# Reordering the first attention batch, tile 0's stores and tile 1's plan in a fused attention and feed-forward kernel

## The chip, the cores and the metric

The kernel runs on one core of one Trainium2 chip. The metric is device time in microseconds of that core. The engines are TensorE (PE; its weight loads are a row of their own, PEld), VectorE (DVE), ScalarE (ACT), GpSimd (POOL) and SyncE (SP), which here only issues DMAs. POOL and ACT issue some DMAs too.

## The reference

Sliding-window attention for 8 batches of 8 heads, 576 positions of 64 features, is followed by a two-layer feed-forward network with a tanh GELU:

```python
scores = scale * np.matmul(q, k.transpose(0, 1, 3, 2))
mask = np.abs(pos[:, None] - pos[None, :]) <= 32
scores = np.where(mask, scores, -1000000000.0)
scores = scores - np.max(scores, axis=-1, keepdims=True)
attn = np.exp(scores)
attn = attn / (np.sum(attn, axis=-1, keepdims=True) + 1e-09)
attn_out = np.matmul(attn, v)                       # (8, 8, 576, 64)
x = attn_out.transpose(0, 2, 1, 3).reshape(4608, 512)
h = x @ w_in                                        # 512 -> 2048
g = 0.5 * h * (1.0 + np.tanh(c * (h + 0.044715 * h * h * h)))
return g @ w_out                                    # 2048 -> 512, float32
```

All inputs and the output are float32; the products on PE are made in float16.

## The kernel before, in words

**Tiles.** The 4608 tokens of the network are cut into nine tiles of 512, counted by `t`. Tile `t` reads the end of batch `t - 1` and the beginning of batch `t` from a ring buffer `xT`, and the attention of batch `b = t + 1` is woven into tile `t`, most of it into its second matrix product. Batch 0 comes first, by itself.

**Attention of one batch.** There are four groups `g = 0..3`, one for each pair of heads, over most of the query positions, and a "tail" group (4, written `-1` when it is done one tile later) for the last positions of all heads. The steps of a group have one letter each in the plans: `s` scores and exp (`score`, PE L415, ACT L427), `m` multiply by the band (DVE L433), `v` sums and products with V (`weigh`: PE L438 and L448, then ACT L473 and L474, a Ln and an Exp that make the reciprocal of the sum), `x` the scaled write into `xT` (`spread`, DVE L483 or L489). For batch 1, `n` and `p` are the sums and the products of two groups at once, `d` copies a chunk of V to the paired layout (`pair_chunk`, DVE L198 and L200), `w` and `u` cast chunks of w_out, `c` is a `combine` (see below).

**Order.** The order on every engine is the order in which the program issues the instructions; nothing is rescheduled. `PLAN_0`, `PLAN_1` and `PLAN` say which attention step is put ahead of which matmul `i` of the second matrix product of tile 0, tile 1 and the rest ("@0" and "@1" name the PSUM tile S0 or S1 that a step uses).

**Feed-forward of one tile.** `ffn_in(t, fc)` makes one of 16 hidden columns with four matmuls (PE L520, out to one of a few PSUM banks) and calls `gelu` (ACT L528). From tile 1 on, the second product is done by a Strassen-Winograd scheme: `sums` (DVE L563) makes four combinations of GELU's outputs after every fourth column, `combine` (DVE L553) makes the combinations T1 to T4 of w_out once, and `ffn_out` runs 112 matmuls (PE L618). Its first product needs eight GELU outputs of every second column. Tile 0 uses a plain product (`ffn_out_0`, PE L592, w_out cast in L218); its four results of 128 tokens (`t4` = 0..3) are copied out of PSUM in L598 and put into the list `later` in the order 0, 3, 1, 2. Results 0 and 1 go to halves of one tile `yo2`, which is in the pool `hp` with the tag "qt16"; `hp` has one buffer for each tag. Results 2 and 3 go to two buffers "yo". ACT stores 0 and 3 to HBM at `i` = 61 and 62, POOL stores 1 and 2 after the loop (L582).

**Batch 2 in tile 1.** `load_qk(2)` puts q and k on SP's queue. `cast_and_turn(2)` casts q on DVE (L343), issues its transposing DMA from SP (L346), then casts k (L367), issues two more transposing DMAs (L369) and the four loads of V (L375), and does combine 2 before the keys and 3 and 4 after them. It returns `rest`, which is called in five steps after columns 9 to 13: four casts of the query tail on ACT into `qt16` (L351, also tag "qt16" of `hp`), the key tail on ACT (L357), and two transposing DMAs and a load on SP. POOL casts V chunk by chunk (`cast_v`, L294), issued after columns 3 to 6. The loads of batch 3 follow on SP.

**The start.** Batch 0 is cast and transposed on PE, pair by pair (`turn`, `trans_out`), with idle matmuls (`spin`, L240) between. `sums_of` makes the sums and reciprocals of a group; `times` multiplies by V for the slots it is given, where slots 0 to 3 are chunks of V and 4 to 7 pair the halves of two neighbours (7 holds the tail). The last chunk is cast by POOL, and ACT and DVE copy halves of it (L730, L729). Then w_in is cast (L218) and the first `ffn_in` starts.

Of the kernel before, what the change touches and what calls it, by code (L numbers as in the profile page):

```python
# [36 lines left out]
def cut(b):  # L37
# [14 lines left out]

PLAN_0 = {8: "r2@0", 10: "s0@1", 11: "w1", 14: "s1@0", 18: "t-1@1", 21: "r3@1", 22: "m0 s2@0", 25: "s3@1", 26: "m1",
          29: "s-1@0", 30: "w2", 31: "m2", 32: "m3", 33: "n0@1", 36: "m-1", 38: "n2@0", 42: "d0", 43: "d1", 44: "v-1@1",
          46: "w3", 48: "x-1", 49: "d2", 51: "d3", 54: "p0@0", 55: "u3 p2@1 x0 x1", 56: "x2 x3", 60: "c1"}
PLAN_1 = PLAN | {10: "s0@0", 12: "s1@1", 33: "s2@0", 40: "v0@1 v1", 50: "x0", 53: "x1", 58: "s-1@1", 62: "s3@0 v2",
                 64: "m-1", 66: "m3", 74: "v-1@1", 76: "x2", 80: "x-1", 86: "s4@1", 91: "v3", 98: "m4"}
PLAN_1[16] = "m0 m1"
for i in (4, 44, 84):
    del PLAN_1[i]  # L60
PAIR_1 = {17: slice(0, 4), 40: slice(4, 8)}

# [9 lines left out]
def kernel(  # L72
# [132 lines left out]
    def stage_w():  # L205
        return stage.tile([128, 4, 512], FP32, name="wst", tag="stage")

    def load_w_in(i, w, c0=0, c1=4):
        nc.sync.dma_start(w[:, c0:c1, :], w_in_v[:, c0:c1, 512 * i:512 * i + 512])  # L209
        return w  # L210
# [17 lines left out]
    vs(4, 0, 1, 2, 3)  # L228
    wi = []
    for i in range(4):  # L230
        wi.append(load_w_in(i, stage_w(), 0, 2))
        load_w_in(i, wi[i], 2, 4)

    idle = KTs[1][:, 0, 0:512]
    nc.vector.memset(idle, 0.0)
# [99 lines left out]
    def cast_and_turn(b):  # L335
        cast_open(b)
        q16, k16 = halfs[b]
        qr, kr, qt, kt = raws[b]
        qt16 = hp.tile([16, NPAIR, 4, 2, 64], FP16, name="qt16", tag="qt16")
        kt16 = hp.tile([64, NPAIR, 2, 64], FP16, name="kt16", tag="t16")  # L340
        def queries(src, dst, p0, p1):
            for pr in range(NPAIR):
                nc.vector.tensor_copy(  # L343
                    dst[:, pr, :, :, :].rearrange("p j h d -> p h j d"),
                    src[:, 2 * pr:2 * pr + 2, :].rearrange("p h (j d) -> p h j d", j=4))
            nc.sync.dma_start_transpose(QTs[b].rearrange("d r j p -> d (r j) p")[:, :, p0:p1],  # L346
                                        dst.rearrange("p r j h d -> p (r j h d)"))

        def rest(i):
            if i < NPAIR:  # L350
                nc.scalar.copy(qt16[:, i, :, :, :].rearrange("p j h d -> p h j d"),  # L351
                               qt[:, 2 * i:2 * i + 2, :].rearrange("p h (j d) -> p h j d", j=4))
            if i == 3:
                nc.sync.dma_start_transpose(QTs[b].rearrange("d r j p -> d (r j) p")[:, :, 128:144],
                                            qt16.rearrange("p r j h d -> p (r j h d)"))
            if i == 4:
                nc.scalar.copy(kt16.rearrange("p r h d -> p (r h d)"), kt.rearrange("p h d -> p (h d)"))  # L357
                nc.sync.dma_start_transpose(
                    KLs[b % 2], kt16.rearrange("p r h d -> p (r h d)"))
                raws[b].append(tailp.tile([64, H, 64], FP32, name="vt", tag="vt"))  # L360
                nc.sync.dma_start(raws[b][4], v[b, :, 512:S, :].rearrange("h p d -> p h d"))

        queries(qr, q16, 0, 128)
        if b == 2:
            combine(2, nc.vector)
        for pr in range(NPAIR):
            nc.vector.tensor_copy(k16[:, pr, :, :, :], kr[:, :, 2 * pr:2 * pr + 2, :])  # L367
            if pr % 2:
                nc.sync.dma_start_transpose(  # L369
                    KTs[b % 2][:, pr - 1:pr + 1, :].rearrange("d r (c p) -> d (r c) p", c=4),  # L370
                    k16[:, pr - 1:pr + 1, :, :, :].rearrange("p r c h d -> p (r c h d)"))
        if b == 2:
            vr = rawp.tile([128, 4, H, 64], FP32, name="qr")
            for c in range(4):
                nc.sync.dma_start(vr[:, c, :, :],  # L375
                                  v[b, :, 128 * c:128 * c + 128, :].rearrange("h p d -> p h d"))
        if b == 2:
            combine(3, nc.vector)
            combine(4, nc.vector)
            raws[b] = [None, None, None, vr]  # L380
            return rest
        queries(qt, qt16, 128, 144)
        nc.vector.tensor_copy(kt16.rearrange("p r h d -> p (r h d)"), kt.rearrange("p h d -> p (h d)"))
        nc.sync.dma_start_transpose(
            KLs[b % 2], kt16.rearrange("p r h d -> p (r h d)"))
# [296 lines left out]
    cast_early(0, 0, split)  # L682
    turn(0)
    trans_out(0, 0, *pts[0], nc.scalar.copy)
    cast_tails(0, nc.vector, odd)
    spin(3)
    trans_tails(0, psO.tile([128, 8, 128], FP16, name="pt", tag="O"), odd, nc.scalar.copy)
    cast_early(0, 1, split)
    spin(1)
    score(0, 0, 0)  # L690
    turn(1)
    cast_early(0, 2, split)
    trans_out(0, 1, *pts[1], nc.scalar.copy)
    spin(1)
    turn(2)
    cast_early(0, 3, split)
    trans_out(0, 2, *pts[2])
    score(0, 1, 1)
    cast_vt(0)
    sums_of(0)  # L700
    spin(1)
    score(0, 2, 0)
    turn(3)
    trans_out(0, 3, *pts[3])
    score(0, 3, 1)
    sums_of(1)
    cast_v(0, 0)
    cast_v(0, 1)
    pair_chunk(0, 0, nc.vector.tensor_copy)
# [7 lines left out]

    cast_v(0, 2)
    pair_chunk(0, 2, nc.vector.tensor_copy)
    sums_of(2)  # L720
    os[0], os[1] = bank(0), bank(1)
    s0 = psS.tile([128, 2, 512], FP32, name="ps_o", tag="S0")
    os[2], os[3] = s0[:, 0, :], pieces("S1", "ps_o")
    spin(2, 512, s0[:, 1, :])
    for g in range(3):
        times(0, g, os[g], groups[(0, g)], (0, 1, 2, 4, 5))
    spin(1, 512, s0[:, 1, :])
    cast_v(0, 3)
    nc.vector.tensor_copy(Vs[0][odd, 7, :, :], raws[0][3][odd, 3, :, :])  # L729
    nc.scalar.copy(Vs[0][even, 6, :, :], raws[0][3][even, 3, :, :])  # L730
    sums_of(3)
    times(0, 3, os[3], groups[(0, 3)], (0, 1, 2, 4, 5))
    spin(3, 512, s0[:, 1, :])
    for g in range(4):
        times(0, g, os[g], groups.pop((0, g)), (3, 6, 7))
        spread(0, g, os[g], lts[g])
    for c in range(4):
        cast_w(wi[0], w_in16[:, :, 0:512], (3,), (c,))
    spin(2, 512, pieces("D", "spin"))
    cast_w(wi[1], w_in16[:, :, 512:1024], (0, 2))  # L740
    for dc in range(2):
# [51 lines left out]
    for t in range(NT):  # L793
        b = t + 1
        att = b < B
        if t:
            for fc in range(begun):
                ffn_in(t, fc, 3, 4, then=False)
            for fc in range(begun):
                gelu(t, fc)  # L800
            if att and b > 1:
                rest = cast_and_turn(b)
            for fc in range(begun, NF):
                ffn_in(t, fc)
                if t == 1 and fc in (3, 4, 5, 6):
                    cast_v(2, fc - 3)
                if t == 1 and 9 <= fc < 14:
                    rest(fc - 9)
                if t == 1 and fc == 8:
                    trans_tails(1, psO.tile([128, 8, 128], FP16, name="pt", tag="O"))  # L810
                if t > 1 and fc == 8 and att:
                    pair_v(b, nc.vector.tensor_copy)
        plan = PLAN_0 if not t else PLAN_1 if t == 1 else PLAN if att else {5: "v-1", 31: "x-1"} if t == B - 1 else {}

        def group(g):
            return (b, g) if g >= 0 else (b - 1, 4)
# [6 lines left out]
        for i in range(113 if t else 65):  # L823
# [3 lines left out]
            for act in plan.get(i, "").split():  # L827
# [33 lines left out]
                elif kind == "u":  # L861
                    cast_w(wo[g], w_out16[:, 12:16, :], on_dve=(3,), cs=(2, 3))
                    cast_tails(1, nc.gpsimd)
                    load_qk(2)
                elif kind == "c":
                    if g == 1:
                        B12 = combine_w()
                    combine(g, nc.vector)
                elif kind == "s":
                    score(*group(g), at)  # L870
                elif kind == "d":
                    pair_chunk(b, g, nc.vector.tensor_copy)
                elif kind == "m":
                    mask(*group(g))
                elif kind == "v":
                    bb, gg = group(g)
                    o, d = weigh(bb, gg, at)
                    ods[g] = (o, invert(bb, gg, d))
                    if t and g < 0 and b + 1 < B:
                        load_vt(b + 1)  # L880
                    if t and g == (3 if att else -1):
                        load_table(gelu_set)
                else:
                    spread(*group(g), *ods[g])
            if t == 1 and i == 30:
                cast_vt(2)
            if t == 1 and i in PAIR_1:
                pair_v(2, nc.vector.tensor_copy, PAIR_1[i])
            if t == 0 and i in (61, 62):
                store(0, *later.pop(0), slice(0, 512), nc.scalar)  # L890
            if t == 0 and i < 64:
                ffn_out_0(*ORDER_0[i])
            elif t and i < 112:
                ffn_out(t, i)
        if t == 0:
            for t4, yo in later:
                store(0, t4, yo)
            wino_rest(B12)
            load_table(gelu_set)
        else:  # L900
            ffn_last(t)
# [31 lines left out]
```

## Time and profile before

| | us |
|---|---|
| median of 13 runs | 304.63 |
| lowest, highest run | 301.81, 306.49 |
| the profiled execution's own time | 304.63 |
| its span, first to last instruction | 302.9 |
| PE busy | 289.6 (96%) |
| DVE busy | 193.2 (64%) |
| ACT busy | 193.8 (64%) |
| POOL busy | 91.3 (30%) |

The profile is one execution. "Busy" counts the engine's own instructions, not the waits on DMAs or the issuing of them. A line of a timeline gives start, duration, engine, source line, operation, output and input, the number of instructions merged, and in brackets the idle time ahead of it with what ended it. "SPq" and "ACTq" are DMA issues on these engines' queues. The first `ffn_in` begins at 19.7 us, tile 0's second product at 35.4, tile 1 at 57.8, tile 1's second product at 71.8 and tile 2 at 91.2.

### The profile page before, as it was taken

The page shows a single profiled execution, that of the slowest core. Times are in us where ns is not written, and L with a number is a line of the kernel's source. Part 1 is how long each engine was busy: PE and PEld are TensorE (multiplying, and loading weights), DVE is VectorE, ACT ScalarE, POOL GpSimd, SP SyncE. Part 2 cuts the span into 40 slices and gives each one's busy share as a digit, 9 for nine tenths or more (in the row PEclk, how much of TensorE's full clock was granted, in tenths as well). Part 3 has the DMA queues.
Part 4 walks back from the last instruction along what each step waited for, and adds up shares of the span by engine and source line. Part 5 has one row for each costly group of instructions (what it writes and reads, how often), then busy time and mean ns, then how long its engine had stood idle before and what let it go on. Part 6 is the DMA issues. An engine that isn't in the chain of part 4 may idle for free.

```text
span 302.9 us, 7124 instructions
## 1 busy us (share of the span) xinstructions
PE 289.6 (96%) x2898; PEld 180.0 (59%) x2898; DVE 193.2 (64%) x434; ACT 193.8 (64%) x307; POOL 91.3 (30%) x142
## 2 busy tenths in 40 slices
PE   8899899899999999999999999999997999999993
PEld 3444443446674488448844884488546864784583
DVE  4554556969768686958685869576955635543452
ACT  4776778389775796579657956695666666706600
POOL 3446426201626050605080506050800050015000
PEclk9999999999999999999999999999999999999998
DMA  7999999999799999799979997999594031004013
GB/s 217 247 358 376 329 267 268 275 250 193 204 186 170 168 240 151 147 153 230 160 153 145 229 160 166 139 228 161 86 172 45 3 92 49 2 3 137 2 40 99
DMA packets 116550, 50.73 MB, mean 167 GB/s; under 512 B 97911, under 2 KB 109943, under 8 KB 116518
## 3 DMA queue, kind: packets, MB, share of 16 engines
q1 hardware_dynamic: 87332, 37.88, 60.0%
q0 software_dynamic: 27776, 10.83, 25.4%
q10 hardware_dynamic: 1410, 1.58, 1.6%
q8 instruction: 22, 0.36, 0.5%
q14 instruction: 10, 0.08, 0.1%
HBM read 36.70 MB, written 9.44 MB: 152 GB/s over the span
## 4 chain that ended last, share of the span: by engine, by line
PE 68%; DMA 18%; SPq 7%; DVE 3%; POOL 1%; issue 1%; ACT 0%
PE mm L618 30%; PE mm L520 17%; PE ph L520 13%; DMA wst<-in_moe_w_out_dram 6%; DMA wst<-in_moe_w_in_dram 4%; DMA KT<-k 3%; PE ps_s L415 3%; SPq L175 2%; PE ps_d L438 2%; DMA kr<-in_k_dram 2%; DMA qr<-in_v_dram 2%; SPq L151 2%; SPq L209 2%; DMA tr<-in_k_dram 2%; PE ps_o L448 2%
## 5 line engine op out<-in xcount | busy, mean ns | idle before, releaser
L520 PEld LDWEIGHTS <-w_in 128*128 128x128 f16 x576 | 56.2, 98 | 66.6 <-POOL w_in L218 0.6
L520 PE MATMUL mm<-xT,w_in 128*128 128x512 f16 x304 | 74.7, 379 | 0.1
L528 ACT ACTIVATE gT<-mm 128x512 f16<-128x512 f32 x76 | 45.2, 598 | 38.9 <-PE mm L520 38.2
L520 PE MATMUL ph<-xT,w_in 128*128 128x512 f16 x272 | 68.2, 379 | 0.1
L582 POOL DMA_DIRECT2D out_dram<-y x55 | 32.9, 605 | 90.4 <-DVE y L647 81.7
L618 PEld LDWEIGHTS <-s 128*128 128x128 f16 x512 | 49.5, 98 | 6.0
L563 DVE TENSOR_TENSOR s<-gT 128x512 f16<-128x512 f16 x64 | 27.2, 425 | 34.2 <-ACT gT L528 34.1
L528 ACT ACTIVATE gT<-ph 128x512 f16<-128x512 f32 x68 | 37.9, 599 | 13.5 <-PE ph L520 13.5
L618 PE MATMUL mm<-t,s 128*128 128x256 f16 x376 | 45.1, 273 | 0.0
L618 PEld LDWEIGHTS <-gT 128*128 128x128 f16 x384 | 35.8, 98 | 6.7
L427 ACT ACTIVATE pe<-ps_s 128x960 f16<-128x960 f32 (+1 forms) x32 | 30.5, 976 | 14.0 <-PE ps_s L415 13.9
L618 PE MATMUL mm<-w_out,gT 128*128 128x256 f16 x256 | 33.2, 273 | 0.0
L97 ACT ACT_TABLE_LOAD x17 | 21.8, 1283 | 2.2 <-issue 1.9
L474 ACT ACTIVATE lt<-lt 128x480 f32<-128x480 f32 (+3 forms) x36 | 21.1, 585 | 1.1
L473 ACT ACTIVATE lt<-ps_d 128x480 f32<-128x480 f32 (+2 forms) x28 | 15.5, 554 | 7.9 <-PE ps_d L438 4.6
L433 DVE TENSOR_TENSOR pe<-pe,band 128x960 f16<-128x960 f16 x28 | 18.8, 695 | 1.1 <-ACT pe L427 1.1
L183 POOL DMA_DIRECT2D V<-in_v_dram x20 | 17.9, 909 | 1.4 <-PE ps_o L448 1.0
L448 PEld LDWEIGHTS <-V 128*64 128x64 f16 x520 | 14.0, 111 | 6.5 <-DVE V L200 1.2
L618 PE MATMUL mm<-t,gT 128*128 128x256 f16 x128 | 16.5, 273 | 0.0
L415 PE MATMUL ps_s<-QT,KT 64*64 64x128 f16 (+3 forms) x576 | 13.8, 216 | 2.4 <-DMA KT<-k 1.8
L415 PEld LDWEIGHTS <-KT 64*64 64x64 f16 x576 | 10.1, 106 | 8.6 <-issue 4.9
L618 PE MATMUL mm<-w_out,s 128*128 128x256 f16 x120 | 14.4, 273 | 0.0
(107 smaller groups left out, 325.3 us busy)
## 6 DMA issues: line engine op xcount, KB each, us to landing
kr<-in_k_dram SPq DMA_DIRECT2D x31, 256.0 KB, 10.9
qr<-in_q_dram SPq DMA_DIRECT2D x6, 1024.0 KB
wst<-in_moe_w_in_dram SPq DMA_DIRECT2D x8, 512.0 KB, 9.3
wst<-in_moe_w_out_dram SPq DMA_DIRECT2D x3, 1024.0 KB, 10.7
V<-in_v_dram POOLq DMA_DIRECT2D x20, 128.0 KB, 8.4
vr<-in_v_dram SPq DMA_DIRECT2D x8, 256.0 KB, 5.4
qr<-in_q_dram SPq DMA_DIRECT2D x7, 256.0 KB, 4.3
out_dram<-y POOLq DMA_DIRECT2D x6, 192.0 KB, 6.1
```

The source lines that it names most:

```text
L97: nc.scalar.add_instruction(mybir.InstLoadActFuncSet(name=nc.get_next_instruction_name(), act_func_set_id=which, ins=[], outs=[]))
L183: nc.gpsimd.dma_start(V[:, c, :, :], v[b, :, 128 * c:128 * c + 128, :].rearrange("h p d -> p h d"))
L415: nc.tensor.matmul(ps[64 * half:64 * half + 64, h, 4 * n * r:4 * n * r + 4 * n].rearrange("k (j p) -> k j p", j=4)[:, :, p0 - q0:p1 - q0], ...
L427: nc.scalar.activation(pe, ps[:, :, 0:w], AF.Exp, scale=SCALE)
L433: nc.vector.tensor_tensor(pe, pe, m.rearrange("k (o j) p -> k o j p", o=1).broadcast_to(list(pe.shape)), op=ALU.mult)
L448: nc.tensor.matmul(o[64 * h:64 * h + 64, cols].rearrange("d (j p) -> d j p", j=4)[:, :, p0 - q0:p1 - q0], Vs[b % 2][:, slot, 2 * pr + h, : ...
L474: nc.scalar.activation(lt[:, 0:n], lt[:, 0:n], AF.Exp, scale=-1.0)
L520: nc.tensor.matmul(ph, w_in16[:, dc, fc * 128:fc * 128 + 128], xT[:, dc, t * 512 % RING:t * 512 % RING + 512], start=(dc == 0), stop=(dc = ...
L528: nc.scalar.activation(gTs[t][:, fc, :], phs[fc], AF.Gelu_apprx_tanh)
L563: nc.vector.tensor_tensor(dst, x, y, op=op)
L582: eng.dma_start(out_v[b, j, q0 + p:q0 + p + e, cols], yo[m:m + e, cols])
L618: nc.tensor.matmul(pys["apart"][:, 0:256] if apart else py[:, blk, :], lhsT, wino[w][:, f, :], start=(new and i % (8 if one else 16) == 0) ...
```

## The change

Seven edits are made together.

1. The first attention: scores are issued ahead of some copies, sums later, and the products with V in three steps (slots 0, 1, 4; then 2, 5; then 3, 6, 7); fewer idle matmuls; DVE casts the last chunk and copies its half from the cast V. One chunk of the first w_in cast goes from POOL to ACT.
2. The loads of w_in are written as a loop.
3. `PLAN_0`: `d2` and `d3` come ahead of `x-1`.
4. `cast_and_turn(2)`: combine 3 comes ahead of the keys; the keys, their transposes, the loads of V and combine 4 come after column 3; `qt16` and `kt16` are allocated when first used.
5. `cast_v` of batch 2 comes after columns 6 to 9 and not 3 to 6.
6. Tile 0's stores come in tile 1: ACT's two after columns 5 and 6, POOL's two after column 7.
7. `PLAN_1`: `s-1`, `m-1` and `v-1` one step earlier; `v3` ahead of the tail's score `s4`, and the GELU table's load after that score's exp.

```diff
 PLAN_0 = {8: "r2@0", ...
-          46: "w3", 48: "x-1", 49: "d2", 51: "d3", 54: "p0@0", 55: "u3 p2@1 x0 x1", 56: "x2 x3", 60: "c1"}
-PLAN_1 = PLAN | {10: "s0@0", 12: "s1@1", 33: "s2@0", 40: "v0@1 v1", 50: "x0", 53: "x1", 58: "s-1@1", 62: "s3@0 v2",
-                 64: "m-1", 66: "m3", 74: "v-1@1", 76: "x2", 80: "x-1", 86: "s4@1", 91: "v3", 98: "m4"}
+          46: "w3", 48: "d2", 50: "d3", 52: "x-1", 54: "p0@0", 55: "u3 p2@1 x0 x1", 56: "x2 x3", 60: "c1"}
+PLAN_1 = PLAN | {10: "s0@0", 12: "s1@1", 33: "s2@0", 40: "v0@1 v1", 50: "x0", 53: "x1", 57: "s-1@1", 62: "s3@0 v2",
+                 63: "m-1", 66: "m3", 73: "v-1@1", 76: "x2", 80: "x-1", 86: "v3", 90: "s4@1", 98: "m4"}
 PLAN_1[16] = "m0 m1"
-for i in (4, 44, 84):
+for i in (4, 44, 84, 91):
     del PLAN_1[i]
...
     for i in range(4):
-        wi.append(load_w_in(i, stage_w(), 0, 2))
-        load_w_in(i, wi[i], 2, 4)
+        wi.append(stage_w())
+        for c0 in (0, 2):
+            load_w_in(i, wi[i], c0, c0 + 2)
...
-        qt16 = hp.tile([16, NPAIR, 4, 2, 64], FP16, name="qt16", tag="qt16")
-        kt16 = hp.tile([64, NPAIR, 2, 64], FP16, name="kt16", tag="t16")
+        small = {}
+        def tails_of(which):
+            if which not in small:
+                small[which] = hp.tile([16, NPAIR, 4, 2, 64], FP16, name="qt16", tag="qt16") if which == "q" else \
+                    hp.tile([64, NPAIR, 2, 64], FP16, name="kt16", tag="t16")
+            return small[which]
...
         def rest(i):
+            qt16, kt16 = tails_of("q"), tails_of("k") if i == 4 else None
...
+        def keys():
+            for pr in range(NPAIR):
+                nc.vector.tensor_copy(k16[:, pr, :, :, :], kr[:, :, 2 * pr:2 * pr + 2, :])
+                if pr % 2:
+                    nc.sync.dma_start_transpose(...)
+            if b == 2:
+                vr = rawp.tile([128, 4, H, 64], FP32, name="qr")
+                for c in range(4):
+                    nc.sync.dma_start(vr[:, c, :, :],
+                                      v[b, :, 128 * c:128 * c + 128, :].rearrange("h p d -> p h d"))
+                raws[b] = [None, None, None, vr]
         queries(qr, q16, 0, 128)
         if b == 2:
             combine(2, nc.vector)
-        for pr in range(NPAIR):
-            ...
-        if b == 2:
             combine(3, nc.vector)
-            combine(4, nc.vector)
-            raws[b] = [None, None, None, vr]
-            return rest
+            return keys, rest
+        keys()
...
     cast_early(0, 0, split)
     turn(0)
     trans_out(0, 0, *pts[0], nc.scalar.copy)
+    cast_early(0, 1, split)
     cast_tails(0, nc.vector, odd)
     spin(3)
-    trans_tails(0, psO.tile([128, 8, 128], FP16, name="pt", tag="O"), odd, nc.scalar.copy)
-    cast_early(0, 1, split)
-    spin(1)
+    trans_tails(0, psO.tile([128, 8, 128], FP16, name="pt", tag="D"), odd, nc.scalar.copy)
     score(0, 0, 0)
     turn(1)
     cast_early(0, 2, split)
-    trans_out(0, 1, *pts[1], nc.scalar.copy)
+    trans_out(0, 1, *pts[1])
     spin(1)
+    sums_of(0)
+    cast_early(0, 3, split)
     turn(2)
-    cast_early(0, 3, split)
+    score(0, 1, 1)
     trans_out(0, 2, *pts[2])
-    score(0, 1, 1)
     cast_vt(0)
-    sums_of(0)
     spin(1)
     score(0, 2, 0)
     turn(3)
     trans_out(0, 3, *pts[3])
+    sums_of(1)
     score(0, 3, 1)
-    sums_of(1)
+    sums_of(2)
...
-    sums_of(2)
     os[0], os[1] = bank(0), bank(1)
     s0 = psS.tile([128, 2, 512], FP32, name="ps_o", tag="S0")
-    os[2], os[3] = s0[:, 0, :], pieces("S1", "ps_o")
-    spin(2, 512, s0[:, 1, :])
+    os[2] = s0[:, 0, :]
     for g in range(3):
-        times(0, g, os[g], groups[(0, g)], (0, 1, 2, 4, 5))
-    spin(1, 512, s0[:, 1, :])
-    cast_v(0, 3)
-    nc.vector.tensor_copy(Vs[0][odd, 7, :, :], raws[0][3][odd, 3, :, :])
+        times(0, g, os[g], groups[(0, g)], (0, 1, 4))
+    sums_of(3)
+    os[3] = pieces("S1", "ps_o")
+    times(0, 3, os[3], groups[(0, 3)], (0, 1, 4))
+    spin(3, 512, s0[:, 1, :])
+    for g in range(4):
+        times(0, g, os[g], groups[(0, g)], (2, 5))
+    cast_v(0, 3, nc.vector.tensor_copy)
+    nc.vector.tensor_copy(Vs[0][odd, 7, :, :], Vs[0][odd, 3, :, :])
     nc.scalar.copy(Vs[0][even, 6, :, :], raws[0][3][even, 3, :, :])
-    sums_of(3)
-    times(0, 3, os[3], groups[(0, 3)], (0, 1, 2, 4, 5))
-    spin(3, 512, s0[:, 1, :])
     for g in range(4):
         times(0, g, os[g], groups.pop((0, g)), (3, 6, 7))
         spread(0, g, os[g], lts[g])
     for c in range(4):
-        cast_w(wi[0], w_in16[:, :, 0:512], (3,), (c,))
+        cast_w(wi[0], w_in16[:, :, 0:512], (3,), (c,), (1,))
...
             if att and b > 1:
-                rest = cast_and_turn(b)
+                parts = cast_and_turn(b)
             for fc in range(begun, NF):
                 ffn_in(t, fc)
-                if t == 1 and fc in (3, 4, 5, 6):
-                    cast_v(2, fc - 3)
+                if t == 1 and fc == 3:
+                    parts[0]()
+                    combine(4, nc.vector)
+                if t == 1 and fc in (5, 6):
+                    store(0, *later.pop(0), slice(0, 512), nc.scalar)
+                if t == 1 and 6 <= fc < 10:
+                    cast_v(2, fc - 6)
+                if t == 1 and fc == 7:
+                    while later:
+                        store(0, *later.pop(0))
                 if t == 1 and 9 <= fc < 14:
-                    rest(fc - 9)
+                    parts[1](fc - 9)
...
                     score(*group(g), at)
+                    if t == 1 and g == 4:
+                        load_table(gelu_set)
...
-                    if t and g == (3 if att else -1):
+                    if t > 1 and g == (3 if att else -1):
                         load_table(gelu_set)
...
-            if t == 0 and i in (61, 62):
-                store(0, *later.pop(0), slice(0, 512), nc.scalar)
...
         if t == 0:
-            for t4, yo in later:
-                store(0, t4, yo)
             wino_rest(B12)
```

More of the change, by code (lines that the diff above doesn't have):

```diff
@@ L361, in rest @@
                 nc.sync.dma_start(raws[b][4], v[b, :, 512:S, :].rearrange("h p d -> p h d"))
+        def keys():
+            for pr in range(NPAIR):
+                nc.vector.tensor_copy(k16[:, pr, :, :, :], kr[:, :, 2 * pr:2 * pr + 2, :])
+                if pr % 2:
+                    nc.sync.dma_start_transpose(
+                        KTs[b % 2][:, pr - 1:pr + 1, :].rearrange("d r (c p) -> d (r c) p", c=4),
+                        k16[:, pr - 1:pr + 1, :, :, :].rearrange("p r c h d -> p (r c h d)"))
+            if b == 2:
[4 more added lines that the diff above has]
+                raws[b] = [None, None, None, vr]
         queries(qr, q16, 0, 128)
@@ L365, in cast_and_turn @@
             combine(2, nc.vector)
-        for pr in range(NPAIR):
[L367 to L371, printed above, removed]
-        if b == 2:
[L373 to L377, printed above, removed]
             combine(3, nc.vector)
-            combine(4, nc.vector)
-            raws[b] = [None, None, None, vr]
-            return rest
+            return keys, rest
+        keys()
+        qt16, kt16 = tails_of("q"), tails_of("k")
         queries(qt, qt16, 128, 144)
```

## The prediction, made before the changed kernel was run

> **What bounds the kernel now.** I read the page first, then TensorE's waits, then the order of time on each queue around the edits.
>
> ```profile
> PE 289.6 (96%) x2898; PEld 180.0 (59%) x2898; DVE 193.2 (64%) x434; ACT 193.8 (64%) x307; POOL 91.3 (30%) x142
> ```
>
> TensorE (PE) is busy 96% of a span of 302.9 us, so only what moves PE counts. The list of PE's waits is short:
>
> ```profile
> PE ps_s L415 <- DMA KT<-k: 1.8, 1, 1.8
> PE spin L240 <- DVE KT L235: 1.3, 1, 1.3
> PE ps_od L448 <- DVE V L200: 0.8, 1, 0.8
> PE mm L592 <- DVE w_out L218: 0.8, 1, 0.8
> PE ps_s L415 <- DVE xT L489: 0.6, 1, 0.6
> ...
> PE ps_od L448 <- DVE V L193: 0.5, 1, 0.5
> ```
>
> The columns are total us, times, longest. V L200 (at 54.25) is what the moved `d2`, `d3` serve. V L193 (78.52) and xT L489 (87.38) lie in tile 1, where the PLAN_1 edits are. With pet L433 (0.16, at 84.85) tile 1 idles 1.25 us. That bounds what the edits can give: 0.8 + 1.25, and a little at the start.
>
> The timelines of three queues in tile 1's first half decide the case. POOL:
>
> ```profile
> 59.76 1.38 POOL L582 DMA_DIRECT2D out_dram<-yo  x2 [4.37 <-DVE yo L598]
> 72.86 0.63 POOL L294 CAST V<-qr 128x512 f16<-128x512 f32 x1 [11.72 <-DMA qr<-in_v_dram]
> 75.00 0.62 POOL L294 CAST V<-qr 128x512 f16<-128x512 f32 x1 [1.51 <-DMA qr<-in_v_dram]
> ```
>
> Two of tile 0's output stores go out at 59.76; only behind them POOL waits, 11.72 us, for batch 2's V. SyncE shows why V is late:
>
> ```profile
> 60.87 5.24 SPq L346 DMA_TRANSPOSE QT<-q  x1
> 66.21 2.63 SPq L369 DMA_TRANSPOSE KT<-k  x2
> 68.89 5.04 SPq L375 DMA_DIRECT2D qr<-in_v_dram  x4
> ```
>
> V is issued behind transposes that take SyncE until 68.84. And ScalarE:
>
> ```profile
> 66.83 0.60 ACT L528 ACTIVATE gT<-ph 128x512 f16<-128x512 f32 x1 [0.49 <-PE ph L520]
> 67.32 0.60 ACT L351 CAST qt<-qt 16x512 f16<-16x512 f32 x1
> 67.83 0.58 ACT L528 ACTIVATE gT<-mm 128x512 f16<-128x512 f32 x1
> 68.32 0.60 ACT L351 CAST qt<-qt 16x512 f16<-16x512 f32 x1
> ```
>
> From 66.83 ScalarE has no slack: GELU and the query-tail casts (L351) alternate every 0.5 us until 72.88, and PE follows.
>
> **What the skill says.** "TensorE: Matmul & The Clock Gate", Architectural detail: ScalarE, VectorE and GpSimd execute strictly in order; only PE pulls weight loads forward. The trace agrees: POOL did nothing between 61.14 and 72.86. The same page, Part 1: after about 3.4 us idle PE falls to half clock and needs as long to recover. The first warming matmuls took 634 ns against 376 ns later. "DMA: Bandwidth & Descriptors", Anatomy of one DMA: about 2.0 us plus bytes/436e3, so an estimated 2.6 us for a 256 KB store; the trace's stores of 256 KB took 5.6 to 6.1 us, of 240 KB 4.4 and of 224 KB 3.3, and I use the trace.
>
> **The change, part by part.**
>
> *First attention (to 19.7 us).* Spins are filler. Scores and sums go ahead of copies; the products with V are split so that only slots 3, 6, 7 wait for the last chunk. That chunk lands at 17.2; ScalarE's half-copy L730 ran only at 17.83, behind four Ln/Exp pairs. With group 3's pair earlier, it can start at 17.2, and VectorE casts the chunk in 0.43 instead of POOL's 0.87. The last products could start some 0.5 us before 18.48. The weights land at 18.57 anyway. From 19.71 PE runs without a gap to 35.39, where it waits 0.81 us for w_out's first cast; that one waited for its DMA. So 0.5 us gained only makes that wait 1.3. I count zero; its cover is the load stream of 0 to 40 us (DMA busy tenths 7 to 9). Without that cover it is -0.5, and if the new order is clumsy, up to +0.5 before the 0.81 us wait is used up. The w_in loop issues the same eight loads in the same order: zero. ScalarE takes one 0.6 us cast from POOL before its GELU table load, with 1.82 us idle behind that: zero.
>
> *`d2`, `d3` ahead of `x-1`.* Four VectorE copies of 0.29 us or more no longer stand behind xT L489, which waited 2.87 us for ScalarE. V's chunks were cast by 50.7, so PE's 0.82 us wait goes; next is w_out's last chunk, cast at 54.1 and needed about 55. Gain 0.8 at this point.
>
> *combine(3) ahead, keys and combine(4) after fc 3.* VectorE stood idle 2.46 us until batch 2's keys landed at 64.39. Now combine(3) (1.2 us) and the first four sums (1.8) fill that; the four key casts begin at 64.4 to 64.8. Their two transposes stand behind the query transpose, which occupies SyncE to 66.11, so the four V loads go out at 68 to 69 as before: zero, -1 to +1.
>
> *The four stores of tile 0.* Two leave ScalarE at 57.75 (0.39 and 0.42 us of issue, after 1.3 of waiting) for fc 5 and 6, about 64 us, where ScalarE has gaps of 0.27 per step: zero to +0.5. The other two leave POOL's 59.76 for fc 7, and there `cast_v(2, 0)` and `cast_v(2, 1)` stand ahead of them in POOL's queue. Those wait for V. This is the step that decides.
>
> `yo2`, which holds t4 = 0 and 1, and `qt16` share the tag "qt16" of a pool with one buffer. `rest(0)` on ScalarE (L351, after fc 9) is the first writer of the new `qt16`, so it must wait until both stores out of `yo2` have landed. Before, they landed by about 65.9, and L351 ran at 67.32 at once. Now:
>
> - V chunk 1 lands at 75.0, as before (stores gone from the traffic at 58 to 65 against two at 64 to 66; 73 to 76.5).
> - Its cast 0.62, handover 0.05: the store of t4 = 1 goes out at 75.7.
> - It lands 4.4 us later, at 80.1: the 240 KB row, since only another store and V's rest are in flight (3.3 to 6.1).
> - L351 starts at 80.1, not 67.32: **12.8 us** late.
>
> Behind L351 on ScalarE are GELUs 10 to 15, four more tail casts and the exp table load. PE runs ahead to fc 12 and stops at about 69: fc 13 needs the PSUM bank of GELU 10. The L618 products need GELU 14, which comes ten instructions, 5 us, after L351 in both kernels. So PE loses the 12.8 whole; its own time gained before (the 0.8 above) only lengthens the wait. VectorE's sums and SyncE's tail transposes and loads of batch 3 wait with it; SyncE's loads still land ahead of their use, since that moved too.
>
> PE idles some 11 us, so it comes back at half clock: fc 13 to 15 and the first products at double time, an estimated 1.4 us (0 to 2).
>
> *Tile 1's order.* `v3` at 86, `s4@1` at 90, `s-1`, `m-1`, `v-1` one step earlier. No instruction is added; the table load stays behind the last exp. V has long landed, so 0.50 goes; the score no longer waits for x-1's read of its bank, so 0.59 goes, and 0.16 with it: -1.25 (0 to -1.25; what may come next is `v3` waiting for `x2`, which ended at 85.99 where `v3` starts near 86.6).
>
> **Sum**: 12.8 + 1.4 - 1.25 = +12.95 on the profiled execution, 304.63 around a span of 302.9, which is also the median of the runs: 317.6. Ends: V chunk 1 at 73, store 3.3, no cold clock: L351 at 77.0, +9.7 - 1.25 = 8.4, 313.1. V at 76.5 and store 6.1: L351 at 83.3, +16 + 2 - 0.6, 322.
>
> **Rivals.**
>
> *Faster: the stores get out in time.* If the store of t4 = 1 lands before ScalarE reaches L351, nothing stalls and the gains stand: 0.8 + 1.25 = 2.05, 302.6. It needs V's second chunk cast by about 62, 13 us earlier than now, or a `qt16` that doesn't wait for `yo2`. Against: SyncE's query transpose alone ends at 66.1. The case decides at L351's start: each us past 67.3 costs one, and at 69.3 the gains are used up.
>
> *Half the stall.* V comes much earlier, because without stores in the traffic both transposes and loads are quicker: the query transpose took 3.51 us in tile 2 instead of 5.24. V chunk 1 at 70.5, store 3.3: L351 at 74.5, +7.2 - 1.25 = 5.9, 310.5. For: the DMA engines were full at 60 to 65. Against: V took 5.7 us to land at a time without stores.
>
> *It doesn't do what it says.* The weights' loop changes nothing issued, and the start is hidden behind the loads. If the stall were absent and `d2`, `d3` only uncovered w_out's cast, the rest would be 304 to 305.
>
> **How the numbers follow.** The measurement can tell about 0.5%, 1.5 us. Forecast 0.80; half stall 0.12; no stall and faster 0.06; no visible effect 0.02. Slower 0.92, same 0.02, faster 0.06. The likeliest is 317.6; from 310.5 to 322 leaves out the faster cases, half of the short stall and what lies above.
>
> **What the profile should show.** POOL's stores of `yo` at about 75.7, behind the second V cast. L351's first cast near 80 with some 13 us idle before it. No PE matmul for about 11 us from 69 on, then L520 matmuls of over 600 ns. No wait for V L200 at 53 to 55. The tile 1 waits gone. From tile 2 on, everything shifted by one constant. I am wrong if L351 starts below 70, or if V's loads are issued before 66.

## The result and the profile after

| | before | changed |
|---|---|---|
| median of the runs, us | 304.31 (48 runs) | 313.22 (11 runs) |
| lowest, highest | 301.81, 307.98 | 312.28, 314.37 |
| ratio, 95% interval | | 1.0295 [1.0268, 1.0321] |

The change makes the kernel 8.9 us slower. Ratios are taken over the runs that lie within 1.5% of the fastest of the same kernel, so a ratio can differ a little from that of the medians. A second profile of the changed kernel (`e1_changed_again`, 312.17 us, span 310.4) is read below, because the first (317.12 us, span 315.4) took longer than any of the runs: in it PE also fell to half clock in tile 6, which the last section shows. That second profile is 7.5 us longer than the profile before.

First the engines' busy time, from its page:

```profile
PE 290.9 (94%) x2894; PEld 180.2 (58%) x2894; DVE 193.7 (62%) x436; ACT 194.5 (63%) x307; POOL 90.4 (29%) x140
```

PE's busy time has hardly grown (289.6 before), its share has fallen by two points. So PE waits more. Its list of waits, and under it ScalarE's (total us, times, longest):

```profile
PE mm L530 <- ACT gT L538: 8.9, 1, 8.9
PE mm L458 <- DVE V L200: 1.3, 1, 1.3
...
PE ps_s L425 <- DVE xT L493: 0.5, 1, 0.5
PE ps_s L425 <- DMA KT<-k: 0.3, 1, 0.3
```

```profile
ACT qt L359 <- DMA out_dram<-yo: 9.7, 1, 9.7
```

One wait of 8.9 us is new, PE for a GELU, and behind it one of 9.7 us, ScalarE for the DMA of a store. (Lines of the changed kernel are mostly ten higher than before: L530 is L520, L538 is L528, L592 is L582, L493 is L483, L499 is L489; L359 is L351.) The 1.3 for V L200 lies in the first attention, at 15 us; the one at 54 is gone. In tile 1 the waits for V L193 and for xT L489 (L499 now) are gone; the 0.5 for xT L493 is a new one.

The three timelines around it, POOL, ScalarE and PE:

```profile
71.91 0.61 POOL L295 CAST V<-qr 128x512 f16<-128x512 f32 x1 [15.88 <-DMA qr<-in_v_dram]
73.12 0.61 POOL L295 CAST V<-qr 128x512 f16<-128x512 f32 x1 [0.59 <-DMA qr<-in_v_dram]
73.67 1.29 POOL L592 DMA_DIRECT2D out_dram<-yo  x2
```

```profile
66.42 0.60 ACT L538 ACTIVATE gT<-ph 128x512 f16<-128x512 f32 x1 [0.49 <-PE ph L530]
76.72 0.62 ACT L359 CAST qt<-qt 16x512 f16<-16x512 f32 x1 [9.70 <-DMA out_dram<-yo]
77.24 0.58 ACT L538 ACTIVATE gT<-mm 128x512 f16<-128x512 f32 x1
```

```profile
67.95 1.03 PE L530 MATMUL ph<-xT,w_in 128*128 128x512 f16 x4
77.87 3.49 PE L530 MATMUL mm<-xT,w_in 128*128 128x512 f16 x8 [8.90 <-ACT gT L538]
81.20 1.03 PE L530 MATMUL ph<-xT,w_in 128*128 128x512 f16 x4
```

Read from top to bottom: POOL does nothing for 15.88 us until V lands, casts two chunks, and only then issues the two stores, at 73.67 and not at 59.76. ScalarE, finished with column 9 at 67, stands until the first of them has landed. PE stops after column 12. When it resumes, eight matmuls take 3.49 us; the next four take 1.03, as ever. The windows show why (busy us of PE, PEld, DVE, ACT and POOL, then PE's clock and the DMA share):

```profile
69.00:77.80 8.80, 0.00 (x0) 0.00 (x0) 0.00 (x0) 1.08 (x3) 3.63 (x6) 0.80 0.87 193
77.80:81.20 3.40, 3.33 (x9) 1.13 (x8) 1.52 (x4) 3.40 (x8) 0.00 (x0) 0.51 0.02 5
81.20:84.00 2.80, 2.80 (x39) 1.75 (x41) 1.07 (x3) 2.44 (x4) 0.00 (x0) 1.00 0.27 47
```

PE had no instruction for 8.8 us, then ran at clock 0.51 for 3.4 us.

The difference to the profile before adds up as follows.

| | before | changed | difference |
|---|---|---|---|
| first tail cast starts | 67.32 | 76.72 | +9.40 |
| from it to the first product, L618 / L628 | 4.49 | 5.34 | +0.85 |
| from that to tile 2's first completed product (chain of work) | 19.54 | 18.40 | -1.14 |
| from there to the end of the span | 211.55 | 209.94 | -1.61 |
| sum | | | +7.50 |

The last row is not the change's: tile 6 of the profile before waits 1.8 us for a key transpose, this one does not (its 0.3 us lies elsewhere), while the first profile of the same changed kernel waits 1.9 us there. Without this row the sum is 9.1 us, near the 8.9 of the medians.

### The profile page after: what moved, and what is told of

Same layout as the page of the kernel before. It is cut to its first block, busy times and chain, and to the rows that moved or that the text cites. A ratio compares the mean times of both kernels' runs of the same rounds, so it can differ in the third digit from the quotient of the medians.

```text
span 315.4 us, 7121 instructions
## 1 busy us (share of the span) xinstructions
PE 291.9 (93%) x2894; PEld 180.3 (57%) x2894; DVE 194.4 (62%) x436; ACT 194.2 (62%) x307; POOL 90.8 (29%) x140
## 4 chain that ended last, share of the span: by engine, by line
PE 68%; DMA 18%; SPq 7%; DVE 3%; POOL 1%; ACT 1%; issue 1%; DVEq 0%; ACTq 0%; POOLq 0%
PE mm L628 30%; PE mm L530 17%; PE ph L530 13%; DMA wst<-in_moe_w_out_dram 5%; DMA wst<-in_moe_w_in_dram 4%; PE ps_s L425 3%; DMA KT<-k 3%; SPq L175 2%; PE ps_d L448 2%; DMA kr<-in_k_dram 2%; SPq L209 2%; SPq L151 2%; PE ps_o L458 2%; DMA tr<-in_k_dram 2%; DMA qr<-in_v_dram 1%; DMA out_dram<-yo 1%
## 5 line engine op out<-in xcount | busy, mean ns | idle before, releaser
L530 PEld LDWEIGHTS <-w_in 128*128 128x128 f16 x576 | 56.6, 99 | 78.0 <-issue 12.8
L530 PE MATMUL mm<-xT,w_in 128*128 128x512 f16 x304 | 76.4, 385 | 9.5 <-ACT gT L538 9.4
L538 ACT ACTIVATE gT<-mm 128x512 f16<-128x512 f32 x76 | 45.1, 597 | 40.2 <-PE mm L530 39.4
L530 PE MATMUL ph<-xT,w_in 128*128 128x512 f16 x272 | 69.1, 382 | 0.1
L592 POOL DMA_DIRECT2D out_dram<-y x55 | 32.9, 607 | 89.0 <-DVE y L657 80.4
L628 PEld LDWEIGHTS <-s 128*128 128x128 f16 x512 | 49.4, 98 | 6.0
L538 ACT ACTIVATE gT<-ph 128x512 f16<-128x512 f32 x68 | 38.0, 600 | 14.8 <-PE ph L530 14.8
L628 PE MATMUL mm<-t,s 128*128 128x256 f16 x376 | 45.1, 273 | 0.0
L628 PEld LDWEIGHTS <-gT 128*128 128x128 f16 x384 | 36.4, 99 | 7.5 <-issue 0.5
L437 ACT ACTIVATE pe<-ps_s 128x960 f16<-128x960 f32 (+1 forms) x32 | 30.4, 975 | 14.3 <-PE ps_s L425 14.2
L628 PE MATMUL mm<-w_out,gT 128*128 128x256 f16 x256 | 34.3, 279 | 0.0
L483 ACT ACTIVATE lt<-ps_d 128x480 f32<-128x480 f32 (+2 forms) x28 | 15.5, 555 | 9.0 <-PE ps_d L448 5.1
L628 PE MATMUL mm<-t,gT 128*128 128x256 f16 x128 | 16.5, 273 | 0.0
L425 PEld LDWEIGHTS <-KT 64*64 64x64 f16 x576 | 10.2, 107 | 8.4 <-issue 4.7
L843 POOL COPY after<-KL 128x1 f16<-128x1 f16 x5 | 1.9, 371 | 44.3 <-DMA KL<-kt 44.3
```

The costliest lines, as they stand in the source:

```text
L425: nc.tensor.matmul(ps[64 * half:64 * half + 64, h, 4 * n * r:4 * n * r + 4 * n].rearrange("k (j p) -> k j p", j=4)[:, :, p0 - q0:p1 - q0], ...
L437: nc.scalar.activation(pe, ps[:, :, 0:w], AF.Exp, scale=SCALE)
L530: nc.tensor.matmul(ph, w_in16[:, dc, fc * 128:fc * 128 + 128], xT[:, dc, t * 512 % RING:t * 512 % RING + 512], start=(dc == 0), stop=(dc = ...
L538: nc.scalar.activation(gTs[t][:, fc, :], phs[fc], AF.Gelu_apprx_tanh)
L592: eng.dma_start(out_v[b, j, q0 + p:q0 + p + e, cols], yo[m:m + e, cols])
L628: nc.tensor.matmul(pys["apart"][:, 0:256] if apart else py[:, blk, :], lhsT, wino[w][:, f, :], start=(new and i % (8 if one else 16) == 0) ...
```

## The experiments

The theory is a chain of two links: POOL's stores stand behind casts that wait for V, and `yo2`, which they read, is the buffer that `qt16` needs. Rivals: V itself is late because its loads were moved with the keys; the new place of the stores hurts through traffic; the start or the plans cost.

**The changed kernel again**, unedited.

> The changed kernel once more, for a second profile beside the first one, which was slower (317.1) than the median (313.2). Theory (POOL's order): the first tail cast L359 starts 7 to 10 us later than the 67.3 of before, its wait ends with the landing of the store of yo, and PE's gap ahead of column 13 is that long; about 313. Rival (cold clock a second time): the first profile was longer because PE also fell to half clock after the key transpose's wait at 240 us; then tile 6 takes 30.5 to 32.3 us here without it, and the distance from tile 2's start to the end is that of the kernel before.

Measured: 313.26 us, ratio 1.0313 [1.0259, 1.0367], the profile above. The tail cast is 9.4 us late and the gap is 8.9, as the theory has it. Tile 6 takes 30.4 us (222.57 to 252.98 on the chain), against 34.0 in the first profile, so the rival on the longer first profile holds as well.

**Stores ahead of the casts.** This cuts the first link.

```diff
-                if t == 1 and 6 <= fc < 10:
-                    cast_v(2, fc - 6)
-                if t == 1 and fc == 7:
+                if t == 1 and fc == 6:
                     while later:
                         store(0, *later.pop(0))
+                if t == 1 and 6 <= fc < 10:
+                    cast_v(2, fc - 6)
```

> The changed kernel with POOL's two stores of tile 0 issued after column 6, ahead of the four casts of V and not between the second and third; nothing else moves. Theory (POOL's order): the stores go out at about 63, land by 67 to 69, L359 waits 0 to 2 us, the whole loss goes: 301.5 to 304.5. Rival (late V: moving the keys behind column 3 delays V and with it tile 1): V lands as late as in the changed kernel, so 309 to 313. Rival (the stores' new place itself, later traffic): 305 to 309.

Measured: 305.11 us, 1.0056 [1.0032, 1.008]. Most of the loss goes, so V's lateness by itself is not the cause: in this profile V's second chunk was cast at 75.96, later than in the changed kernel. But it stays above the expected range. From the timelines of POOL, ScalarE and PE:

```profile
59.36 1.45 POOL L592 DMA_DIRECT2D out_dram<-yo  x2 [3.27 <-DVE yo L608]
```

```profile
62.81 0.38 ACTq L592 DMA_DIRECT2D out_dram<-yo  x1
...
70.72 0.62 ACT L359 CAST qt<-qt 16x512 f16<-16x512 f32 x1 [3.69 <-DMA out_dram<-yo]
```

```profile
71.88 3.17 PE L530 MATMUL mm<-xT,w_in 128*128 128x512 f16 x8 [2.89 <-ACT gT L538]
```

POOL issues at 59.36 and not at 63: nothing in POOL's order ties the stores to PE's column 6. What still holds the tail cast for 3.69 us is ScalarE's own store of result 0, the other half of `yo2`, issued at 62.81; it took 7.8 us to land. PE waits 2.89 us for it and comes back at half clock (0.50 granted from 71.9 to 73.0). In the changed kernel the same store, issued at 62.80, took 4.8 us at the most, so that alone it would have held the cast for less than 1 us; the wait for POOL's store covers it.

**Another buffer.** This cuts the second link and leaves POOL's order alone.

```diff
-            yo = pys["yo"][:, t4, :] if t4 < 2 else yp.tile(...)
+            yo = pys["yo"][:, t4 // 3, :] if t4 in (0, 3) else yp.tile(...)
```

> The changed kernel with results 0 and 3 (ACT's stores) in the two halves of yo2 and results 1 and 2 (POOL's stores) in the yo buffers, which nothing reuses. POOL's order stays as it is, its stores still go out at about 74. Theory (POOL's order meets the reuse of the buffer): L359 waits for ACT's stores alone, issued at 63 and 64, and starts at 67 to 69.5: 302 to 306. Rival (POOL's lateness hurts by itself, through V or the store traffic): still 311 to 314.

Measured: 303.44 us, 0.9993 [0.9971, 1.0015]. POOL and ScalarE:

```profile
74.68 1.29 POOL L592 DMA_DIRECT2D out_dram<-yo  x2
```

```profile
69.52 0.62 ACT L359 CAST qt<-qt 16x512 f16<-16x512 f32 x1 [1.88 <-DMA out_dram<-yo]
```

POOL's stores are as late as in the changed kernel, and the loss is gone: nobody needs those buffers, and the traffic of late stores does no harm that shows. The wait left, 1.88 us, is for ScalarE's stores, which this edit puts both into `yo2`; that fits a ratio of 0.9993 where the version with the stores put back, below, has 0.993 and 0.9948. So neither of the two links costs much alone; it takes both.

**The stores alone**, in the kernel before.

```diff
-            if t == 0 and i in (61, 62):
-                store(0, *later.pop(0), slice(0, 512), nc.scalar)
...
-            for t4, yo in later:
-                store(0, t4, yo)
...
-                if t == 1 and fc in (3, 4, 5, 6):
-                    cast_v(2, fc - 3)
+                if t == 1 and fc in (5, 6):
+                    store(0, *later.pop(0), slice(0, 512), nc.scalar)
+                if t == 1 and 6 <= fc < 10:
+                    cast_v(2, fc - 6)
+                if t == 1 and fc == 7:
+                    while later:
+                        store(0, *later.pop(0))
```

> The kernel before with only the four stores and the four V casts moved as in the change (stores after columns 5, 6 and 7, casts after columns 6 to 9, qt16 allocated at first use); keys, plans and the first attention as before. Theory (POOL's order): the loss is here in full, V lands at 75 as before and not at 73.7, so 313 to 317, slightly more than the changed kernel. Rival (the loss needs the moved keys or the new first attention): 304 to 306.

Measured: 314.57 us over four runs; the ratio, 1.0255 [1.0188, 1.0321], rests on two of them (311.14 and 312.64 us). The loss is there without any other edit; these lines are from the longest of the four runs, 316.96 us, whose tile 1 began 2.6 us later than in the profile before:

```profile
75.89 1.29 POOL L590 DMA_DIRECT2D out_dram<-yo  x2
```

```profile
78.96 0.62 ACT L358 CAST qt<-qt 16x512 f16<-16x512 f32 x1 [8.97 <-DMA out_dram<-yo]
```

It is not clearly larger than the changed kernel's, so that part of the expectation stays open.

**Keeping PE busy through the gap.** Idle matmuls ahead of column 13, first 28, then 40:

```diff
             for fc in range(begun, NF):
+                if t == 1 and fc == 13:
+                    spin(28, 512, pieces("S1", "spin"))      # 40 in the second
                 ffn_in(t, fc)
```

> The changed kernel with 28 idle matmuls (6 us at full clock, into a free PSUM tile) ahead of column 13 of tile 1, so that TensorE works through most of its gap. Theory (the gap also costs a cold clock, put at 1.4 in the prediction and 1.7 in the first profile): columns 13 to 15 run at full clock, 311.3 to 312.2, 1 to 2 us under the changed kernel. Rival (the clock costs nothing, since ScalarE sets the pace there): 313.0 to 313.5.

Measured: 314.49 us, 1.0333 [1.0275, 1.0392], no gain. The tail cast came at 78.25 in this profile, so the idle matmuls left 4.0 us of the gap, and part of the columns ran at half clock again: the run does not test what it was meant to. Hence the longer one.

> The changed kernel with 40 idle matmuls (8.6 us) ahead of column 13 of tile 1 in place of the 28 of the run before, which left 4.0 us idle behind them and columns at half clock all the same. Theory (cold clock): with under 2 us left idle columns 13 to 15 take 0.9 us each and not 1.7, and the first product L628 comes 4.5 us after the first tail cast L359, as in the kernel before, against 5.3 to 6.2 in the changed kernel's profiles. Rival (something else delays L628): still 5.3 or more. The total follows L359's start, so it may be 311 to 315 in both cases; the distance decides.

Measured: 313.19 us, 1.0309 [1.0255, 1.0364]. PE's timeline:

```profile
68.85 8.80 PE L241 MATMUL spin<-KT 128*128 128x512 f16 x40
79.15 2.02 PE L530 MATMUL mm<-xT,w_in 128*128 128x512 f16 x8 [1.50 <-ACT gT L538]
81.15 1.02 PE L530 MATMUL ph<-xT,w_in 128*128 128x512 f16 x4
```

With 1.5 us left idle, the eight matmuls take 2.02 us and not 3.49. The tail cast started at 77.99, the first product at 82.14: 4.15 us, against 5.34 and 6.17 in the two profiles of the changed kernel. So, by these three profiles, the cold clock is worth 1.2 to 2.0 us after the gap. The total does not show it: 313.19 us is the changed kernel's time. In this profile the tail cast came 1.3 us later than in the second profile of the changed kernel, because V's second chunk was cast at 74.37 (at 74.62 with the 28 idle matmuls) and not at 73.12. Whether the idle matmuls delay V or this is chance, the runs do not show.

**The other edits, one by one**, each in the kernel before. The start alone:

> The kernel before with the new first attention alone (with the cast of one chunk of w_in on ACT). Theory (the load stream covers it): the first column product starts 0.5 to 1 us earlier, w_out's first cast stays at 35, the wait ahead of L592 grows by as much, 303.3 to 304.3, no difference. Rival (the start is on the path): 302.8 to 303.3.

Measured: 304.02 us, 0.9994 [0.9974, 1.0013]. The first column product comes at 18.98 (19.71 before), but tile 0's second product at 35.58 (35.39 before). Of the 0.7 us, w_out's wait takes back 0.3, being 1.1 us and not 0.8, and a new wait for a key cast (L287, at 31.9) 0.4:

```profile
PE mm L592 <- DVE w_out L218: 1.1, 1, 1.1
```

With fewer idle matmuls PE also waits 1.2 us for V at 14.6, and its granted clock is 0.50 from 16 to 18 us, where the profile before has 1.00.

The plans alone (edits 3 and 7):

> The kernel before with PLAN_0, PLAN_1 and the table load's new place alone. Prediction's sum: 0.8 (V L200) and 0.6 to 1.25 in tile 1, so 302.0 to 302.6. Theory now (V's arrival in tile 1 sets that stretch, and the first 0.8 only lengthens the wait for V there): the wait at 54 goes, the wait for V L193 grows, 303.0 to 304.0.

Measured: 303.59 us, 0.9955 [0.9925, 0.9985], that is 0.5 to 2.3 us of 304. The interval holds both the prediction's 2.05 and a part of the theory's 0.1 to 1.1; it says that the plans gain, not how much. In the profile (span 300.6) the wait at 54 is gone, and the one for V L193 is 0.19: it did not grow here, as I had supposed it would.

The keys alone (edit 4, with 2 and 5):

> The kernel before with the keys and combine 4 behind column 3, combine 3 ahead of them and the V casts after columns 6 to 9 alone; stores, plans and start as before. Prediction's step: zero, -1 to +1. Theory (V is bound by SP's order, the query transpose first): 303.5 to 304.5. Rival (V a microsecond earlier, 73.7 and not 75.0, helps tile 1): 302.5 to 303.5.

Measured: 304.09 us, 0.9996 [0.9971, 1.002]: zero.

**The stores put back**, everything else of the change kept.

```diff
+            if t == 0 and i in (61, 62):
+                store(0, *later.pop(0), slice(0, 512), nc.scalar)
...
+            for t4, yo in later:
+                store(0, t4, yo)
...
-                if t == 1 and fc in (5, 6):
-                    store(0, *later.pop(0), slice(0, 512), nc.scalar)
-                if t == 1 and fc == 7:
-                    while later:
-                        store(0, *later.pop(0))
```

> The changed kernel with the four stores back where the kernel before had them, all other edits kept. Theory (POOL's order meets the reuse of the buffer, and ACT's later stores add some us behind it): the first tail cast waits for nothing, all of the loss goes, and the gains of the prediction's faster rival stand, 301.5 to 303.0, under both kernels. Rival (moving the keys costs by itself): 304 to 306.

Measured: 302.27 us, 0.993 [0.9904, 0.9957]. ScalarE's tail cast follows the GELU ahead of it at once:

```profile
67.21 0.60 ACT L359 CAST qt<-qt 16x512 f16<-16x512 f32 x1
```

PE's timeline in tile 1 has two waits:

```profile
79.11 0.38 PE L458 MATMUL ps_od<-pe,V 128*64 128x64 f16 x12 [1.19 <-DVE V L193]
82.07 0.23 PE L425 MATMUL ps_s<-QT,KL 64*64 64x96 f16 x2 [0.19 <-DVE xT L493]
```

This version beats both kernels, the one before by 0.4 to 1.0%. It was run once more, beside the same without the new start:

> The same kernel as e8_old_stores, beside e11 on the same chip. 301.8 to 302.8; it stays under the kernel before by 1.3 to 2.9 us (0.43% to 0.96%).

> The changed kernel with the four stores at their old place and the first attention of the kernel before: the plans and the moved keys together. Theory (the start is covered by the loads of weights): as with the new start, 301.8 to 302.8. Rival (the start's earlier columns count once the later waits are gone): 0.5 to 1 above that kernel, 302.8 to 303.5.

Measured: 302.71 us, 0.9948 [0.9926, 0.997], and 302.72 us, 0.9967 [0.9941, 0.9992]. The better version is confirmed. Whether the start adds anything to it, these runs can't tell.

## Why the prediction was right, and where its sizes were off

The direction and the mechanism held: the stores behind two casts on POOL, the shared buffer, L351 late, PE stopped after column 12, the loss whole. Predicted were 317.6 us and +12.95, measured 313.22 and +8.9; the range of 310.5 to 322 held it. That the first profile took 317.12 us is chance: its tile 6 took 34.0 us, against 30.4 in the second. Nearest to what happened is the prediction's own lower end, V at 73, a store of 3.3 us and no cold clock, 313.1. Point by point:

- *The tail cast 12.8 us late.* It was 9.4. Two terms of the sum were too long. "V chunk 1 lands at 75.0, as before": its cast started at 73.12. It started at 74.05 and 74.14 in the start's and the plans' profiles, where stores and keys stand at their old places, at 75.96 with the stores first, at 75.67 with them put back. So the row I took from one profile has a spread of some 3 us of its own, and whether the stores' traffic has a part in it does not show. "It lands 4.4 us later": it took 3.0. The landing times of the stores in the second profile:

```profile
DMA to landing us min/median/max: 3.0/3.2/4.8
```

  I chose the 240 KB row. The Trainium skill's estimate of 2.6 us ("DMA: Bandwidth & Descriptors", Anatomy of one DMA) was nearer for these stores; beside the query transpose and the loads ahead of it the stores of `yo` took 5.6 to 6.1 before, and one took 7.8 in the kernel with the stores first. 75.0 - 73.1 and 4.4 - 3.0 make 3.3 of the 3.4 us.
- *The cold clock, 1.4.* The distance to the first product grew by 0.85 and by 1.68 in the two profiles; keeping PE busy took that away. This agrees with the Trainium skill, "TensorE: Matmul & The Clock Gate", Part 1, in the second profile: half clock after the idle stretch (0.51 granted), full clock some 3.4 us after PE resumed. In the first profile that took 4.9 us.
- *Tile 1's gains, -1.25.* The stretch shrank by 1.14, but the three waits are not the whole account. They are gone, the tail's score `s4` no longer waits for `x-1` (L499), and in their place the score `s-1`, one step earlier now, waits 0.5 us for `x0` (L493), which reads the PSUM tile S1 that it writes. So idle time shrank by 0.75; why PE's busy time in the stretch is 0.3 less (17.74, 18.05 before) does not show. Nor is it shown that the new order removes the wait for V L193: where nothing stalls it is 0.19 with the plans alone, but 1.19 and 0.99 with the stores put back, 0.50 before.
- *ScalarE's stores, "zero to +0.5".* This step failed, hidden by the larger one. Its issue is cheap; what I left out is that one of them reads `yo2` as well, so its landing holds the tail cast once POOL's stores are out of the way: by 3.7 us with the stores first, and by 1.9 where both of ScalarE's stores read that buffer. I had costed the issue and not the buffer.
- *Start and keys, zero.* Held, at 0.9994 and 0.9996, the start not by w_out's wait alone, as its profile shows. (ScalarE's half-copy L730 stood behind three Ln/Exp pairs, not four.)
- *The faster rival, 302.6.* Its number came true in the kernel with the stores put back, 302.27 and 302.71, where nothing stalls. Its sum did not, as far as the profiles show. The 0.8 at 54 is gained, but not the 1.25 in tile 1: the waits there are 1.19 and 0.19 in one profile, 0.99 and 0.29 in the other, and tile 2 begins at 91.16 and 91.29, against 91.35 before. Most of what these profiles gain lies in tile 6 (30.4 us in both, 32.3 before), where the change alters nothing. Without the new start tile 2 began at 89.62. So that the number fits is in part luck, and where the medians' gain arises stays open.
- *The half stall.* Its 310.5 did not occur, but its point, that V and a store can come sooner, made the stall 3.4 us shorter than forecast. In the second profile of the changed kernel the query transpose did take 3.89 us and not 5.24. The 3.51 us that the prediction reads is of tile 3 (issued at 124.02), though; in tile 2 it took 5.46.

## What to carry to other kernels

When a store is moved on an in-order queue, ask what stands ahead of it there and what that waits for, and then who reuses the buffer that the store reads: each alone cost little here, both together 9 us. A store that nobody waits for can be as late as it likes. And a term taken from a single execution, such as a DMA's landing, deserves a range from several rows, quiet and loaded ones apart.

## What the runs showed of the hardware that I had not expected

A short wait can cost the clock too, shorter than the 3.4 us of idling that the prediction reckoned with. In the first profile of the changed kernel PE waited 1.93 us for a key transpose in tile 6 and came back at half clock; these are windows of that profile (columns as above):

```profile
238.00:240.00 2.00, 0.20 (x2) 0.00 (x0) 1.52 (x4) 1.68 (x2) 0.00 (x0) 1.00 1.45 89
240.00:242.00 2.00, 1.87 (x44) 1.39 (x45) 0.00 (x0) 1.41 (x2) 0.00 (x0) 0.62 0.44 99
242.00:244.00 2.00, 2.00 (x12) 1.45 (x10) 0.00 (x0) 1.32 (x3) 0.00 (x0) 0.53 0.00 0
244.00:246.00 2.00, 2.00 (x23) 1.61 (x24) 1.78 (x4) 0.00 (x0) 0.00 (x0) 1.00 0.00 0
```

The kernel before waited 1.84 us at the same place and stayed at clock 1.00. Tile 6 took 34.0 us in the first case and 32.3 in the second, so 1.7 us hung on it.

The other profiles narrow this down. Behind the first attention, waits of PE of 1.1 to 1.84 us left the clock at 1.00, and every one of 1.93 us or more (1.93, 1.98, 2.07, 2.89, 4.0 and the long ones) brought 0.50. In the first attention 1.2 and 1.3 us, among other short waits, were enough. The fall does not come at a fixed distance: it came some 2.1 us after PE's last matmul with the stores first, 5.3 us after it in the second profile of the changed kernel, and with 28 idle matmuls 0.9 us after PE had resumed. But the length is regular. Leaving out the ends of the profiles, there are twelve stretches at half clock in them: eight of 3.4 us, two of 6.8 and two of 10.2. That looks like steps of 3.4 us; what sets where a step begins, the runs do not show.
